# A rebuilt head for a fused attention and expert kernel: loads, first chunk, dummy matmuls and V copies

## The chip, the cores and the metric

The kernel runs on one core of a Trainium2 chip. The metric is the device time of one execution in microseconds (us). Names used below: TensorE (PE) multiplies matrices and writes PSUM, VectorE (DVE) and ScalarE (ACT) do elementwise work, GpSimd (POOL) does elementwise work in SBUF, and SyncE (SP) issues the DMAs.

## The reference

One sequence of S = 2048 tokens of width D = 448 passes a layernorm and a grouped attention (16 query heads of 28, one shared key and value head), and then a second layernorm and a block in which only the 8 tokens with the highest router score go through a gated feed-forward layer.

```python
q = (x @ wq).reshape(B, S, H, Dh).transpose(0, 2, 1, 3)      # x: layernormed, H = 16, Dh = 28
k = x @ wk                                                    # one key head for all 16
v = x @ wv
scores = jnp.einsum("bhqd,bkd->bhqk", q, k) * (Dh ** -0.5)
o = jnp.einsum("bhqk,bkd->bhqd", softmax(scores), v)
h = x0 + o.transpose(0, 2, 1, 3).reshape(B, S, H * Dh) @ wo   # x0: the input
...
r = xl @ w_r                                                  # xl = layernorm(h)
idx = jnp.argsort(-r)[:, :8]
y = (silu(x_sel @ w_gate) * (x_sel @ w_up)) @ w_down * sigmoid(r_sel)
out = h + xl + scatter_add(0, idx, y)
```

## The kernel before

The program is written as a graph of operations with reads, writes, an estimated duration and a priority. A planner (`_Graph.plan`) runs a list schedule over these estimates and so fixes, before anything runs, the order of the instructions on each engine. Each engine then works through its own list strictly in that order; semaphores hold an instruction until what it reads is there. A changed estimate, priority or dependency can therefore reorder all lists.

**Tiles.** x is 16 tiles of 128 tokens (`x_sb`), in four chunks of 512. For each chunk (`chunk(c)`, line 459) VectorE takes mean and variance of each tile (`bn_stats`, `bn_aggr`, lines 464 and 466), the reciprocal root is made (chunk 0: Ln and Exp on ScalarE, lines 471 and 473; others: a power on GpSimd, line 476), VectorE normalises four tiles (`xn`, line 479), TensorE transposes them in pairs (line 352), and the transposed chunk is copied from PSUM to `xnT` (lines 490, 493). Projections follow: K by `wk_rep` (the key weights four times side by side), copied into two versions `K[:, p]` (lines 501, 505), and V by `wv_pad`, copied into `Vs` in five scaled versions, one instruction each (line 516, with `vone` for a column of constants that sums the weights). Chunk 0 also projects Q of block 0 (`q_project`, line 450).

**Blocks.** A block b is 512 queries of 4 heads; there are 16. For each of the 16 key tiles j, a unit is two matmuls of Q and K into two PSUM banks, twice (p = 0, 1). In most tiles ScalarE takes the exponential of each unit (`act_unit`, line 753: `P`), in 57 of 256 tiles VectorE makes an approximation of it (`dve_unit` and `shift`, lines 766 and 772: `Y`). Matmuls with `Vs` add both into the block's accumulator. Block 0 has no VectorE tiles, blocks 4, 8 and 12 have three, the others four. ScalarE has two pairs of score banks to alternate on, and VectorE one, so a score matmul waits for the exponential two units earlier.

**Around the head.** SyncE issues, in this order: x tiles 0, 1 and 2, 3, then wk, wq, wv, x 4 to 15 in three loads, w_r, the three expert weights, and wo in four parts (which wait for each other). GpSimd fills `ident` (for the transposes), spreads wk, wq and wv into padded tiles (`wk_rep`, `wq_pad`, `wv_pad`, lines 391 to 402), and makes many constants. `last_w` (line 654) prepares products of wo and of the last x tiles with w_r, eight VectorE instructions of 448 columns, for the end of the kernel. At the end of a block VectorE copies the accumulator to `Ot` (line 551).

The same graph is also built a second time in an exact form that runs only when a flag asks for it.

Of the kernel before, what the change touches and what calls it, by code (L numbers as in the profile page):

```python
# [230 lines left out]
def _main(nc, G, sb, ps, psb, flag, scr, xs, A_x, A_wq, A_wk, A_wv, A_wo, B_w_r, B_w_gate, B_w_up, B_w_down, out,  # L231
# [13 lines left out]
    VC = (1.0, 1.6796875, 1.4140625, 1.1875, 1.0)  # L245
# [25 lines left out]
    vone = sb("vone", [128, NV, 4, 32], F32)  # L271
# [73 lines left out]
    def pk(b):  # L345
        return ("ps", b)
# [44 lines left out]
    G.op(PO, lambda e: e.memset(wk_rep[:, :, :], 0.0), 530, writes=["wk_rep"])  # L391
    for i in range(4):
        G.op(PO, lambda e, i=i: e.tensor_copy(wk_rep[0:CK, :, 32 * i:32 * i + DH], wk_sb[0:CK, :, :]), 300,
             reads=["wk_sb"], writes=["wk_rep"])
    G.op(PO, lambda e: e.memset(wq_pad[:, :, :, :], 0.0), 1800, writes=["wq_pad"])
    for ch in range(NCH):
        v = wq_pad[0:CK, ch, :, :].rearrange("p g (i c) -> p (g i) c", c=32)[:, :, 0:DH]
        G.op(PO, lambda e, ch=ch, v=v: e.tensor_copy(v, wq_sb[0:CK, ch, :].rearrange("p (h d) -> p h d", d=DH)), 590,
             reads=["wq_sb"], writes=["wq_pad"])
    G.op(PO, lambda e: e.memset(wv_pad[:, :, :], 0.0), 210, writes=["wv_pad"])  # L400
    G.op(PO, lambda e: e.tensor_copy(wv_pad[0:CK, :, 1:1 + DH], wv_sb[0:CK, :, :]), 280,
         reads=["wv_sb"], writes=["wv_pad"])
    G.op(PO, lambda e: e.memset(vone[:, :, :, :], 0.0), 500, writes=["vone"])
    for v in range(NV):
        G.op(PO, lambda e, v=v: e.memset(vone[:, v, :, 0:1], VC[v]), 100, writes=["vone"])  # L405
    G.prio = -1000
    G.op(PO, lambda e: e.memset(wo_pad[:, :, :], 0.0), 1600, writes=["wo_pad"])
# [35 lines left out]
    def head_bank(c):  # L443
        if c > 0:
            return MISC
# [584 lines left out]
```

## Time and profile before

| What | Value |
|---|---|
| Runs of the kernel | 444.52 us median of 3, from 441.43 to 445.93 |
| The profiled execution | 442.73 us |
| Its span (first to last instruction) | 441.3 us |
| TensorE busy | 357.1 us (81%) |
| VectorE busy | 366.5 us (83%) |
| ScalarE busy | 382.1 us (87%) |
| GpSimd busy | 46.8 us (11%) |
| DMA engines, mean busy share of the first three fortieths | 0.8, 0.9, 0.6 |

How to read the lines quoted below. In a timeline row stand start and length in us, engine, line of the kernel, operation, output and input, shapes and a count when like instructions are merged; in brackets the idle time of the engine just before and what ended it. In a group of the page the columns are count, then busy time and mean ns of one, then idle time before and its releasers. In a row of windows stand the stretch, its length, the busy time of each engine with the number of instructions, the granted TensorE clock (1.00 is full), the DMA share and GB/s. In a row of DMA issues stand the tile, the queue, the count, the size and the time from issue to landing. Releasers are inferred.

### The profile page before, as it was taken

To read this page: it belongs to the slowest core of one execution; us is meant where nothing else is said; L and a number is where in the kernel's file an instruction comes from. 1 tells how busy PE (TensorE), PEld (TensorE's weight loads), DVE (VectorE), ACT (ScalarE), POOL (GpSimd) and SP (SyncE) were. 2 spreads that over 40 slices of the span, in tenths; PEclk is the share of its full clock that TensorE was granted. 3 is DMA by queue.
4 is the path that set the end of the run, shared out by engine and by line. 5 is a ranking of instruction groups with operands and counts; after the bars stand their busy time and mean duration, and the time that the engine had idled before them with its cause. 6 is when DMAs were issued, how large, how long until landed. Compare 5 with 4: busy or idle time off the path is not lost.

```text
span 441.3 us, 7932 instructions
## 1 busy us (share of the span) xinstructions
PE 357.1 (81%) x3243; PEld 106.7 (24%) x3243; DVE 366.5 (83%) x792; ACT 382.1 (87%) x425; POOL 46.8 (11%) x76
## 2 busy tenths in 40 slices
PE   0888898888887988989887988888879879887754
PEld 0333212222222222222221222222222212221243
DVE  4999629989788899899986898999988899995371
ACT  1397689999998999999996999999989998996640
POOL 8210001010101101010102110101011010111000
PEclk9998769999999999999998999999999998998955
DMA  8960000000000030000000030000000200000010
GB/s 227 272 186 11 0 1 27 4 26 1 26 3 25 1 94 17 22 8 26 1 24 4 3 108 3 26 3 25 4 25 1 88 24 4 25 7 22 1 43 8
DMA packets 17350, 15.75 MB, mean 36 GB/s; under 512 B 5944, under 2 KB 14428, under 8 KB 17308
## 3 DMA queue, kind: packets, MB, share of 16 engines
q1 hardware_dynamic: 17212, 15.16, 11.8%
q8 instruction: 27, 0.44, 0.4%
q14 instruction: 15, 0.12, 0.1%
q0 software_dynamic: 96, 0.02, 0.0%
HBM read 11.70 MB, written 3.47 MB: 34 GB/s over the span
## 4 chain that ended last, share of the span: by engine, by line
DVE 31%; ACT 29%; PE 25%; DMA 9%; POOL 2%; issue 1%; SPq 1%; POOLq 0%; DVEq 0%
ACT P L753 29%; PE ps L349 25%; DVE Y L766 11%; DVE Y L772 8%; DMA Rb<-l_scr 5%; DVE Ot L551 2%; DMA xnT<-r 2%; POOL On L563 1%; DMA x_sb<-in_A_x_dram 1%; DMA l_scr<-Lc 1%; DVE xn L479 1%; DVE bn L464 1%; DVE K L505 1%; DVE xnT L493 1%; DVE Vs L516 1%
## 5 line engine op out<-in xcount | busy, mean ns | idle before, releaser
L753 ACT ACTIVATE P<-ps 128x1024 bf16<-128x1024 f32 x398 | 370.7, 1082 | 26.3 <-PE ps L349 25.0
L349 PE MATMUL ps<-Q,K 64*128 64x512 bf16 x1024 | 187.0, 394 | 44.0 <-ACT P L753 26.6
L766 DVE TENSOR_SCALAR Y<-ps 128x512 int16<-128x512 f32 x228 | 146.8, 680 | 24.9 <-PE ps L349 24.5
L772 DVE TENSOR_SCALAR Y<-Y 128x2048 int16<-128x2048 int16 x171 | 117.7, 724 | 1.5
L349 PEld LDWEIGHTS ps<-Q,K 64*128 64x128 bf16 x1024 | 44.6, 93 | 191.7 <-ACT P L753 141.4
L349 PE MATMUL ps<-P,Vs 128*32 128x512 bf16 x796 | 81.2, 399 | 0.3 <-ACT P L753 0.3
L349 PE MATMUL ps<-Y,Vs 128*32 128x512 bf16 x912 | 75.2, 387 | 0.5 <-DVE Y L772 0.3
L563 POOL TENSOR_TENSOR On<-Ot,Rb 128x512 bf16<-128x512 f32 x15 | 21.7, 1446 | 280.8 <-DMA Rb<-l_scr 280.8
L349 PEld LDWEIGHTS ps<-P,Vs 128*32 128x32 bf16 x796 | 20.6, 93 | 51.7 <-issue 50.4
L349 PEld LDWEIGHTS ps<-Y,Vs 128*32 128x32 bf16 x912 | 22.7, 96 | 22.8 <-issue 11.5
L349 PE MATMUL ps<-xnT,wq_pad 112*128 112x512 bf16 x64 | 21.8, 437 | 4.0 <-DVE Ot L551 3.5
L349 PE MATMUL ps<-wo_pad,On 128*128 128x448 bf16 (+1 forms) x64 | 18.0, 378 | 8.5 <-POOL On L563 7.7
L551 DVE COPY Ot<-ps 128x512 f32<-128x512 f32 x15 | 10.3, 688 | 8.0 <-PE ps L349 7.6
L456 DVE TENSOR_SCALAR Q<-ps,qone 128x512 bf16<-128x512 f32 x16 | 11.7, 730 | 5.9 <-PE ps L349 5.8
L352 PE MATMUL ps<-ident,xn 128*112 128x128 bf16 x64 | 6.3, 259 | 11.2 <-POOL vone L405 10.6
L464 DVE BATCH_NORM_STATS2 bn<-x_sb 128x6 f32<-128x448 bf16 x16 | 9.3, 602 | 4.4 <-DMA x_sb<-in_A_x_dram 4.4
L585 POOL TENSOR_TENSOR st<-st,nhalf 128x1 f32<-128x1 f32 x12 | 7.7, 641 | 48.1 <-DVE st L583 48.1
L579 DVE TENSOR_TENSOR hbuf<-ps,x_sb 128x448 f32<-128x448 f32 x12 | 7.4, 619 | 4.6 <-PE ps L349 4.5
L349 PEld LDWEIGHTS ps<-wo_pad,On 128*128 128x128 bf16 x64 | 4.7, 100 | 17.7 <-POOL On L563 8.8
L352 PEld LDWEIGHTS ps<-ident,xn 128*112 128x112 bf16 x64 | 5.2, 161 | 13.3 <-POOL vone L405 10.6
L598 DVE SCALAR_TENSOR_TENSOR junk<-hbuf,st,w_rb 128x448 bf16<-128x448 f32 x12 | 8.1, 677 | 0.0
L349 PEld LDWEIGHTS ps<-xnT,wq_pad 112*128 112x128 bf16 x64 | 4.4, 104 | 14.7 <-DVE Ot L551 7.0
(164 smaller groups left out, 158.8 us busy)
## 6 DMA issues: line engine op xcount, KB each, us to landing
Rb<-l_scr SPq DMA_DIRECT2D x15, 256.0 KB
wg_sb<-in_B_w_gate_dram SPq DMA_DIRECT2D x1, 1568.0 KB, 12.0
wu_sb<-in_B_w_up_dram SPq DMA_DIRECT2D x1, 1568.0 KB, 17.6
wd_sb<-in_B_w_down_dram SPq DMA_DIRECT2D x1, 1568.0 KB, 21.1
x_sb<-in_A_x_dram SPq DMA_DIRECT2D x3, 448.0 KB, 6.4
out_dram<-x_sb SPq DMA_DIRECT2D x3, 448.0 KB, 2.9
xn_scr<-xn SPq DMA_DIRECT2D x3, 448.0 KB, 3.9
x_sb<-in_A_x_dram SPq DMA_DIRECT2D x2, 224.0 KB, 2.9
```

Source lines behind the costliest of these rows:

```text
L349: return lambda e: e.matmul(o, lhsT=l, rhs=r, start=start, stop=stop)
L352: return lambda e: e.transpose(o, i, ident[0:p, 0:p])
L456: G.op(DV, lambda e: e.tensor_scalar(Q[:, b % 4, :], ps[:, bank, :], qone[:, 0:1], None, ALU.add), dvt(512), reads=[pk(bank), "qone"], wri ...
L464: G.op(DV, [lambda e, t=t: e.bn_stats(bn6[:, t, :], x_sb[:, t, 0:D])], dvt(D), reads=[("x", t)], writes=[("bn6", t)])
L551: G.op(DV, lambda e: e.tensor_copy(Ot[:, rb, :], ps[:, acc_bank(b), :]), dvt(512), reads=[pk(acc_bank(b))], writes=[("Ot", rb)], prio=u - 30)
L563: G.op(PO, lambda e: e.tensor_tensor(On[:, qb % 2, g, :], Ot[:, rb, :], Rb[:, rb, :], ALU.mult), 1270, reads=[("Ot", rb), ("Rb", rb)], wri ...
L579: G.op(DV, lambda e: e.tensor_tensor(hbuf[:, hr, :], ps[:, bank, 0:D], x_sb[:, t, 0:D], ALU.add), dvt(D), reads=[pk(bank), ("x", t)], writ ...
L585: G.op(PO, lambda e: e.tensor_tensor(st[:, t, 4:5], st[:, t, 7:8], nhalf[:, 0:1], ALU.pow), 570, reads=[("st7", t), "nhalf"], writes=[("st ...
L598: G.op(DV, lambda e: e.scalar_tensor_tensor(junk[:, :], hbuf[:, hr, :], st[:, t, 4:5], w_rb[:, :], ALU.mult, ALU.mult, accum_out=st[:, t, ...
L753: G.op(AC, lambda e: e.activation(P[:, sl, :, :], ps[:, b0:b0 + 2, :], ACT.Exp, bias=EBIAS, scale=OCT), 905, reads=[pk(b0), pk(b0 + 1)], w ...
L766: G.op(DV, lambda e, k=k: e.tensor_scalar(Y[:, n, 0, p + 2 * k, :].bitcast(I16), ps[:, 4 + k, :], 0.0, 32639.0 - 3 * STEP, ALU.max, ALU.mi ...
L772: G.op(DV, lambda e: e.tensor_scalar(Y[:, n, v, :, :].bitcast(I16), Y[:, n, 0, :, :].bitcast(I16), v * STEP, None, ALU.add), 610, reads=[( ...
```

## The change

The first stretch of the kernel is rewritten:

- **Loads.** x tiles 0 to 3 are four loads; then wk, wv and wq; x 4 to 15 wait until tile 3 has landed; wo (four parts, no longer one after the other), w_r and the expert weights wait until tile 15 has landed.
- **Weights.** `wk_rep` and `wv_pad` are cleared by VectorE and filled by ScalarE, in one instruction each; `wq_pad` is filled half by ScalarE and half by GpSimd.
- **Dummy matmuls.** 44 matmuls of `ident` by itself into bank 7, which nothing reads, are TensorE's first instructions.
- **Chunk 0** (`chunk0`) goes in halves of two tiles: Ln and Exp for each half on ScalarE, a transpose and a copy for each tile (half 0 on ScalarE, half 1 on VectorE), K and Q projections of 256 columns, the four K copies and the first Q copy on ScalarE.
- **Chunks 1 to 3.** One or two of four tiles are normalised on GpSimd (`nmean` serves it); chunk 1's root is made on ScalarE; PSUM banks 7, 4 and 5 take turns where bank 7 served alone.
- **V copies.** One instruction multiplies the projected values by the four constants `vcc`; the fifth copy, equal to the first, is gone; the column of constants is written once, on GpSimd.
- **Order.** Some priorities and estimates differ: Q of block 1 and the sum of w_r come later. The planner lays out all lists anew.

```diff
-    dma(x_sb[:, 0:2, 0:D], x_v[:, 0:2, :], [("x", t) for t in range(0, 2)], lat=2600.0)
-    dma(x_sb[:, 2:4, 0:D], x_v[:, 2:4, :], [("x", t) for t in range(2, 4)], lat=2600.0)
+    for t in range(4):
+        dma(x_sb[:, t, 0:D], x_v[:, t, :], [("x", t)], lat=2700.0 + 250 * t)
     dma(wk_sb[0:CK, :, :], A_wk.rearrange("(k p) n -> p k n", p=CK), ["wk_sb"], lat=4000.0)
-    dma(wq_sb[0:CK, :, :], A_wq.rearrange("(k p) n -> p k n", p=CK), ["wq_sb"], lat=6000.0)
-    dma(wv_sb[0:CK, :, :], A_wv.rearrange("(k p) n -> p k n", p=CK), ["wv_sb"], lat=6500.0)
+    dma(wv_sb[0:CK, :, :], A_wv.rearrange("(k p) n -> p k n", p=CK), ["wv_sb"], lat=4000.0)
+    dma(wq_sb[0:CK, :, :], A_wq.rearrange("(k p) n -> p k n", p=CK), ["wq_sb"], lat=5500.0)
     for i in range(4, NT, 4):
-        dma(x_sb[:, i:i + 4, 0:D], x_v[:, i:i + 4, :], [("x", t) for t in range(i, i + 4)], lat=6000.0)
+        dma(x_sb[:, i:i + 4, 0:D], x_v[:, i:i + 4, :], [("x", t) for t in range(i, i + 4)], lat=3500.0 + 400 * i,
+            reads=[("x", 3)])
...
-    G.op(PO, lambda e: e.memset(wk_rep[:, :, :], 0.0), 530, writes=["wk_rep"])
-    for i in range(4):
-        G.op(PO, lambda e, i=i: e.tensor_copy(wk_rep[0:CK, :, 32 * i:32 * i + DH], wk_sb[0:CK, :, :]), 300,
-             reads=["wk_sb"], writes=["wk_rep"])
+    G.op(DV, lambda e: e.memset(wk_rep[:, :, :], 0.0), 300, writes=["wk_rep"])
+    G.op(DV, lambda e: e.memset(wv_pad[:, :, :], 0.0), 100, writes=["wv_pad"])
+    G.op(AC, lambda e: e.activation(wk_rep[0:CK, :, :].rearrange("p k (i c) -> p k i c", c=32)[:, :, :, 0:DH],
+                                    wk_sb[0:CK, :, :].unsqueeze(2).broadcast_to([CK, NCH, 4, DH]), ACT.Identity),
+         500, reads=["wk_sb"], writes=["wk_rep"])
+    G.op(AC, lambda e: e.activation(wv_pad[0:CK, :, 1:1 + DH], wv_sb[0:CK, :, :], ACT.Identity), 200,
+         reads=["wv_sb"], writes=["wv_pad"])
     for ch in range(NCH):
...
+        if ch % 2:
+            G.op(AC, lambda e, v=v, w=w: e.activation(v, w, ACT.Identity), 480, reads=["wq_sb", "wq_pad"],
+                 writes=[("wq_pad", ch)])
+        else:
+            G.op(PO, lambda e, v=v, w=w: e.tensor_copy(v, w), 590, reads=["wq_sb", "wq_pad"],
+                 writes=[("wq_pad", ch)])
...
     for i in range(4):
-        dma(wo_pad[32 * i + 1:32 * i + 1 + DH, :, 0:D], wo_v[i], ["wo_pad"], lat=14000.0)
-    dma(w_rb[:, :], B_w_r.partition_broadcast(128), ["w_rb"], lat=14000.0)
+        dma(wo_pad[32 * i + 1:32 * i + 1 + DH, :, 0:D], wo_v[i], [("wo", i)], reads=[("x", NT - 1), "wo_pad"],
+            lat=6000.0)
+    dma(w_rb[:, :], B_w_r.partition_broadcast(128), ["w_rb"], reads=[("x", NT - 1)], lat=6000.0)
...
+    def v_project(c, bank):
+        pv = ps[:, bank, 0:128].rearrange("p (t c) -> p t c", c=32)
+        G.op(PE, [mm(pv[:, k, :], xnT[0:CK, c, ch, k * 128:(k + 1) * 128], wv_pad[0:CK, ch, :],
+                     ch == 0, ch == NCH - 1) for k in range(4) for ch in range(NCH)], 16 * 28,
+             reads=["wv_pad"] + xk(c), writes=[pk(bank)])
+        G.op(DV, lambda e: e.tensor_tensor(Vs[:, :, 4 * c:4 * c + 4, 1:32],
+                                           pv[:, :, 1:32].unsqueeze(1).broadcast_to([128, NV, 4, 31]),
+                                           vcc[:, :].unsqueeze(2).unsqueeze(3).broadcast_to([128, NV, 4, 31]),
+                                           ALU.mult), 620, reads=[pk(bank), "vcc"], writes=[("V", c)])
+
+    def chunk0():
+        G.prio = -500
+        for _ in range(44):
+            G.op(PE, mm(ps[:, 7, 0:128], ident[:, :], ident[:, :], True, True), 107, reads=["ident"], writes=[pk(7)],
+                 prio=-900)
+        for t in range(4):
...
+            if t % 2:
+                sl = slice(t - 1, t + 1)
+                G.op(AC, lambda e, sl=sl: e.activation(var[:, sl], mv[:, sl, 1], ACT.Ln, bias=EPS), 200,
+                     reads=[("mv", t - 1), ("mv", t)], writes=[("var", t // 2)])
+                G.op(AC, lambda e, sl=sl: e.activation(rstd[:, sl], var[:, sl], ACT.Exp, scale=-0.5), 200,
+                     reads=[("var", t // 2)], writes=[("rstd", -1 - t // 2)])
+        for h in range(2):
+            for t in (2 * h, 2 * h + 1):
...
+                if h == 0:
+                    G.op(AC, lambda e, src=src, dst=dst: e.activation(dst, src, ACT.Identity), 480,
+                         reads=[pk(t)], writes=[("xnT", 0, t)])
+                else:
+                    G.op(DV, lambda e, src=src, dst=dst: e.tensor_copy(dst, src), 340,
+                         reads=[pk(t)], writes=[("xnT", 0, t)])
+            c = slice(256 * h, 256 * h + 256)
+            x2 = [("xnT", 0, 2 * h), ("xnT", 0, 2 * h + 1)]
+            for kind in (("K", "Q") if h == 0 else ("Q", "K")):
+                bank = (4 if kind == "K" else 6) + h
+                G.op(PE, [mm(ps[:, bank, 0:256], wk_rep[0:CK, ch, :] if kind == "K" else wq_pad[0:CK, ch, 0, :],
+                             xnT[0:CK, 0, ch, c], ch == 0, ch == NCH - 1) for ch in range(NCH)], 4 * 115,
+                     reads=(["wk_rep"] if kind == "K" else wqk) + x2, writes=[pk(bank)])
...
+        v_project(0, 5)
+        G.prio = 9
+        q_project(1, MISC)
...
         for t in tl:
...
+            if t % 2 == 0 or t == 7:
+                G.op(DV, lambda e, t=t: e.tensor_scalar(xn[:, t, :], x_sb[:, t, 0:D], mv[:, t, 0:1], rstd[:, t:t + 1],
+                                                        ALU.subtract, ALU.mult), 310,
+                     reads=[("x", t), ("mv", t), ("rstd", c)], writes=[("xn", t)])
+            else:
+                G.op(PO, lambda e, t=t: e.tensor_scalar(xn[:, t, :], x_sb[:, t, 0:D], nmean[:, t:t + 1],
+                                                        rstd[:, t:t + 1], ALU.add, ALU.mult), 700,
+                     reads=[("x", t), ("nm", c), ("rstd", c)], writes=[("xn", t)])
...
-        for v in range(NV):
-            G.op(DV, lambda e, pv=pv, c=c, v=v: e.scalar_tensor_tensor(Vs[:, v, 4 * c:4 * c + 4, :], pv, VC[v],
-                                                                       vone[:, v, :, :], ALU.mult, ALU.add),
-                 dvt(128), reads=[pk(bank), "vone"], writes=[("V", c, v)])
```

More of the change, by code (lines that the diff above doesn't have):

```diff
@@ L400, in _main @@
[L400 to L403, printed above, removed]
+        w = wq_sb[0:CK, ch, :].rearrange("p (h d) -> p h d", d=DH)
+        if ch % 2:
[4 more added lines that the diff above has]
+                 writes=[("wq_pad", ch)])
@@ L404, in _main @@
+    wqk = [("wq_pad", ch) for ch in range(NCH)]
     for v in range(NV):
[L405 to L406 removed]
+        G.op(PO, lambda e, v=v: e.memset(vcc[:, v:v + 1], VC[v]), 100, writes=["vcc"])
+        G.op(PO, lambda e, v=v: e.memset(Vs[:, v, :, 0], VC[v]), 100, writes=["V1"])
+    G.prio = -300
     G.op(PO, lambda e: e.memset(wo_pad[:, :, :], 0.0), 1600, writes=["wo_pad"])
+    wok = [("wo", i) for i in range(4)]
@@ L615, in first_top @@
         first_row(bank)
-    old = [("xnT", 0), ("xnT", 1)]
+    old = xk(0) + xk(1)
     def first_row(bank):
@@ L675, in last_pre @@
             G.op(PE, fns[2 * p:2 * p + 2], 2 * 190,
-                 reads=[("On", 1, g) for g in range(3)] + ["wo_pad", "wo_hi", "wo_lo", "ident", ("x", t)],
+                 reads=[("On", 1, g) for g in range(3)] + ["wo_pad", "wo_hi", "wo_lo", "ident", ("x", t)] + wok,
                  writes=[pk(bank)])
```

161 lines of the change are left out of this document (86 added, 75 removed).

## The prediction

> **What bounds the kernel now.** I read the page first, for the engine that carries the span, then ScalarE's part of the timeline, then the timelines of VectorE and TensorE beside it, then windows with the granted clock.
>
> ```profile
> span 441.3 us, 7932 instructions
> ...
> L753 ACT ACTIVATE P<-ps 128x1024 bf16<-128x1024 f32 x398 | 370.7, 1082 | 26.3 <-PE ps L349 25.0
> ```
>
> ScalarE's 398 exponentials take 370.7 us, 0.931 us apart when nothing holds them (370.7 / 398; the 1082 ns of one overlap). So the span is the start of the first, plus 370.7, plus the gaps between them, plus what follows the last. The timeline of ScalarE gives start and gaps:
>
> ```profile
> 11.70 1.02 ACT L490 ACTIVATE xnT<-ps 112x1024 bf16<-112x1024 bf16 x1 [4.96 <-PE ps L352]
> 15.57 0.78 ACT L501 ACTIVATE K<-ps,kb,ksc 128x512 bf16<-128x512 f32 x1 [2.85 <-PE ps L349]
> 19.81 6.52 ACT L753 ACTIVATE P<-ps 128x1024 bf16<-128x1024 f32 x7 [3.46 <-PE ps L349]
> 26.61 2.16 ACT L753 ACTIVATE P<-ps 128x1024 bf16<-128x1024 f32 x2 [0.27 <-PE ps L349]
> 28.95 4.79 ACT L753 ACTIVATE P<-ps 128x1024 bf16<-128x1024 f32 x5 [0.17 <-PE ps L349]
> 33.99 1.94 ACT L753 ACTIVATE P<-ps 128x1024 bf16<-128x1024 f32 x2 [0.26 <-PE ps L349]
> 38.04 1.02 ACT L753 ACTIVATE P<-ps 128x1024 bf16<-128x1024 f32 x1 [2.11 <-PE ps L349]
> 39.26 2.97 ACT L753 ACTIVATE P<-ps 128x1024 bf16<-128x1024 f32 x3 [0.19 <-PE ps L349]
> 42.80 1.95 ACT L753 ACTIVATE P<-ps 128x1024 bf16<-128x1024 f32 x2 [0.57 <-PE ps L349]
> 45.28 1.94 ACT L753 ACTIVATE P<-ps 128x1024 bf16<-128x1024 f32 x2 [0.53 <-PE ps L349]
> 48.99 1.02 ACT L753 ACTIVATE P<-ps 128x1024 bf16<-128x1024 f32 x1 [1.77 <-PE ps L349]
> 50.21 1.94 ACT L753 ACTIVATE P<-ps 128x1024 bf16<-128x1024 f32 x2 [0.19 <-PE ps L349]
> 53.49 7.58 ACT L753 ACTIVATE P<-ps 128x1024 bf16<-128x1024 f32 x8 [1.34 <-PE ps L349]
> 61.88 2.11 ACT L753 ACTIVATE P<-ps 128x1024 bf16<-128x1024 f32 x2 [0.81 <-PE ps L349]
> 64.81 1.94 ACT L753 ACTIVATE P<-ps 128x1024 bf16<-128x1024 f32 x2 [0.82 <-PE ps L349]
> ...
> 406.52 6.88 ACT L753 ACTIVATE P<-ps 128x1024 bf16<-128x1024 f32 x7 [0.53 <-PE ps L349]
> ```
>
> The first exponential starts at 19.81. Block 0 has 32 of them (16 key tiles, two each, none on VectorE): 27 in the rows up to 50.21, and five of the eight at 53.49, so the 32nd is through at about 58.2. That is 38.4 us for 32 x 0.931 = 29.8 us of work: 8.6 us of gaps. They lie where a new chunk of keys is first needed (the 9th, 17th and 25th exponential: 27.5, 38.04, 48.99) and at 53.49. The last exponential ends at 413.4; the 27.9 us behind it is untouched by the change. VectorE, which makes the chunks, has no rest meanwhile:
>
> ```profile
> 20.18 1.30 DVE L479 TENSOR_SCALAR xn<-x_sb,mv,rstd 128x448 bf16<-128x448 bf16 x4
> 21.49 1.12 DVE L464 BATCH_NORM_STATS2 bn<-x_sb 128x6 f32<-128x448 bf16 x2
> 22.53 0.67 DVE L493 COPY xnT<-ps 112x1024 bf16<-112x1024 bf16 x1
> 26.39 1.49 DVE L505 TENSOR_SCALAR K<-ps,ksc,kb 128x512 bf16<-128x512 f32 x2
> 29.66 1.06 DVE L516 SCALAR_TENSOR_TENSOR Vs<-ps,vone 128x128 bf16<-128x128 f32 x5
> 59.51 0.69 DVE L551 COPY Ot<-ps 128x512 f32<-128x512 f32 x1 [5.82 <-PE ps L349]
> ```
>
> Its first idle time that matters is the 5.82 us before 59.51: until some 53 us VectorE sets the pace, ScalarE after that.
>
> **Term 1, the first exponential.** TensorE's projections of chunk 0 and the loads:
>
> ```profile
> 13.67 1.86 PE L349 MATMUL ps<-xnT,wk_rep 112*128 112x512 bf16 x4 [1.15 <-DVE mv L466]
> 21.43 0.65 PE L352 MATMUL ps<-ident,xn 128*112 128x128 bf16 x8
> 25.21 1.04 PE L349 MATMUL ps<-xnT,wk_rep 112*128 112x512 bf16 x4
> ...
> 0.72 0.95 SPq L363 DMA_DIRECT2D x_sb<-in_A_x_dram  x2
> 2.23 0.48 SPq L363 DMA_DIRECT2D wq_sb<-in_A_wq_dram  x1
> ...
> wq_sb<-in_A_wq_dram SPq DMA_DIRECT2D x1, 392.0 KB, 5.2
> ...
> wk_sb<-in_A_wk_dram SPq DMA_DIRECT2D x1, 24.5 KB, 4.1
> wv_sb<-in_A_wv_dram SPq DMA_DIRECT2D x1, 24.5 KB, 5.0
> ```
>
> SyncE spends 0.48 us on an issue. Four x loads end at 2.6, so wk is issued at 2.6, wv at 3.1, wq at 3.6; by the old times to landing they would be there at 6.7, 8.1 and 8.8. Nothing more lies ahead of them than before, when wq landed at 2.23 + 5.2 = 7.4, and x 4 to 15 now wait for tile 3; I take 6.3, 7.2 and 8.2. ScalarE's order is now: wk_rep, wv_pad, Ln and Exp of half 0, Ln of half 1, two wq_pad chunks, Exp of half 1, two xnT copies. A step that waits for a load holds all behind it. With 0.5 us for a copy of 448 to 512 elements (between half of the 1.02 and the 0.78 above) and 0.25 for a small one: wk_rep to 6.9, wv_pad 7.5, half 0's rstd 8.0, wq_pad 8.2 to 9.2, half 1's rstd 9.45, xnT 10.5. VectorE's xn and TensorE's transposes of half 0 fit in between.
>
> Then four half projections follow (K, Q, Q, K). A whole one took 1.86 us at 13.67 and 1.04 at 25.21; a half is 0.93 or 0.52. At the slow rate they end at 14.3; two K copies on ScalarE follow, and the first exponential is at 15.3. At the fast rate it is 13.65; with the late loads and the slow rate 16.1.
>
> Which rate holds? The page "TensorE: Matmul & The Clock Gate" of the Trainium skill (Part 1, and "Why this matters for your kernels") asks for about 4 us of matmuls to reach full rate, and says that an idle stretch of about 3 us loses it; by it the 44 dummies buy the 1.65 us if the rest between them and the projections stays short. The windows bear on this:
>
> ```profile
> 36.60:40.00 3.40, 1.98 (x28) 0.86 (x26) 3.40 (x7) 1.76 (x2) 0.00 (x0) 1.00 0.00 0
> 40.00:43.40 3.40, 3.27 (x20) 1.43 (x20) 3.40 (x11) 2.83 (x4) 0.00 (x0) 0.50 0.02 5
> ...
> 50.20:63.90 13.70, 12.51 (x57) 2.31 (x56) 2.58 (x7) 11.48 (x12) 0.00 (x0) 0.50 0.01 1
> ...
> 64.00:86.50 22.50, 19.54 (x180) 5.04 (x178) 21.21 (x49) 21.70 (x24) 1.70 (x1) 1.00 0.04 14
> ...
> 1.17 0.56 POOL L375 TENSOR_SCALAR ident<-idi 128x128 bf16<-128x128 int32 x1
> ```
>
> The numbers after the stretch and its length are PE, PEld, DVE, ACT, POOL, granted clock, DMA share and GB/s; the last row is of the timeline. After 3.4 us with TensorE busy 1.98, the granted clock is 0.50. The dummies run from 1.73 (when the last row's ident is done) for 44 x 0.08 to 0.12 us, that is till 5.3 to 7.0 (0.65 / 8; the slow end is half of a slow 256-column pass, 0.93 / 8). Till 10.55 only 16 transposes follow, 1.3 us of work in 3.5. I take the slow rate: **15.3, 4.5 us earlier**, with ends of 3.7 and 6.2. By the page's rule alone it would be 6.2.
>
> **Term 2, the gaps of block 0.** Chunk 1's Ln and Exp sit behind the 2nd and 3rd exponential on ScalarE (0.4 us on the path, new), so its rstd comes at 15.3 + 3 x 0.93 + 0.4 = 18.5. Then VectorE in the planner's new order: three xn (1.0; the fourth is on GpSimd), statistics (0.8), two xnT (1.2), Q of block 1 (0.7), small steps and one bn_stats (0.8), the V copy (0.65), bn_stats (0.6), first K copy (0.7): 25.0. With a score matmul and its semaphore the 9th exponential is at 25.7, against 27.5 before. ScalarE would have been ready at 15.3 + 8 x 0.931 + 0.4 = 23.15, so there is a gap of 2.5 there.
>
> Behind it VectorE has less to do per chunk: one V copy of 128x496 instead of five of 128x128. It is not in the trace; 0.65 is what a 512-column pass costs (1.49 / 2), less would be the five's 1.06 / 5, so it is 0.4 less than before, and at worst the same 1.06. One or two of four xn (0.33 each) go to GpSimd. What is decisive is the order: the new list has the Y steps of block 1 behind chunk 3, where the old had them between chunks (the row at 30.72 below is one). VectorE needs about 6 us from the first K copy of chunk 1 to that of chunk 2, some 31.7, including two of the wo-by-w_r products moved forward (row below); ScalarE needs chunk 2 at 25.7 + 7.4 = 33.1. Chunk 3 comes at 37.6 against 40.6. These two gaps (2.11 and 1.77) go.
>
> ```profile
> 30.72 1.27 DVE L766 TENSOR_SCALAR Y<-ps 128x512 int16<-128x512 f32 x2
> ...
> 67.53 0.62 DVE L656 SCALAR_TENSOR_TENSOR junk<-wo_pad,w_rb 128x448 bf16<-128x448 bf16 x1
> ...
> ...
> L563 POOL TENSOR_TENSOR On<-Ot,Rb 128x512 bf16<-128x512 f32 x15 | 21.7, 1446 | 280.8 <-DMA Rb<-l_scr 280.8
> ```
>
> New waits come instead. TensorE's list has four transposes in a row, two of them of tiles normalised on GpSimd (one tile between the 0.56 that 128 columns took for ident and the 1.45 of a two-input product of 512; if it goes by columns, 0.56 x 448 / 128 = 1.96; I take 0.9), and the scores of the next exponentials queue behind them: 0.4 us a chunk. Block 2's Q projection still blocks TensorE for 1.0 to 1.9, as at 53.49. The eight products of 0.62 now lie ahead of or among the first Y steps; from the first Y to the fifth unit VectorE needs 10.9 us (ten Y at 0.64, four shifts taken alike, a Q copy of 0.7, two products), beside 13 exponentials, 12.1 us. I put 2.0 for all this, between 0.5 and the 8.3 lost before from the 9th to the 32nd (58.2 - 27.5 - 24 x 0.931). So block 0 ends at 25.7 + 24 x 0.931 + 2.0 = 50.0: **8.2 us earlier** than 58.2, term 1 included.
>
> The four wo loads, w_r and the expert weights go behind x 15, about 12 us; the first user, the sum of w_r, is at some 31. SyncE is free again long before Ot of block 0. The POOL memsets that went (wk_rep, wv_pad, vone) hid under the loads.
>
> **Term 3, the rest.** The gaps of 0.81 and 0.82 at 61.88 and 64.81 belong to the stretch at clock 0.50; a full gain is 1.6, none is 0, I take 0.3. From block 2 on the new lists are nearly the old ones, so nothing else moves: 0, plus or minus 2.
>
> **Sum.** 8.2 + 0.3 = 8.5 us. The profiled execution took 442.73, so it would take 434.2. The median of the runs shown is 444.52, 1.8 above it (they reach from 441.43 to 445.93), so I predict **436.0**.
>
> **Rivals.** (a) The gain at the start is handed back at the chunks: the gaps after the 9th exponential stay at 8.3, and only 27.5 - 25.7 = 1.8 is left: 442.7. For it: VectorE was the pace until 53 us, and most of its work remains. Against: the Y steps leave its way. A late wq, with all of ScalarE's queue behind it, gives the same. 0.15.
> (b) The dummies hold the clock, or the loads are early: first exponential 13.65, all of chunk 1 1.6 earlier, only 0.5 of gaps later, and both gaps of term 3 gone: 8.2 + 1.6 + 1.5 + 1.6 = 12.9: 431.6. For it the page's rule above; against it the sparse 3.5 us. 0.18.
> (c) Slower: the clock of 0.50 falls into blocks 1 to 3. In the old kernel its 13.7 us fell at the end of block 0, where TensorE had 57 matmuls in it. A block at full clock has 19.5 us of TensorE in 22.5. A projection takes 1.86 / 1.04 = 1.79 times as long at half clock; midway between that and none, 1.4, makes 27.3, so each us at half clock loses 0.18. Beyond 48 us of it the gain is gone; 90 us would cost 16, net +7.5: 452.0. Against: from 63.9 on the clock was 1.00. 0.05.
>
> **Chances.** Forecast 0.62, (a) 0.15, (b) 0.18, (c) 0.05. About 1%, 4.4 us, is what can be told from no change. Faster: 0.60 of the forecast's and (b), 0.78. Within: (a) and the forecast's poor end, 0.17. Slower: 0.05. Range: 430.5 (all of (b) but its best) to 442.0 (into (a)).
>
> **What would show it.** First exponential near 15.3; chunk 0's half projections 0.93 or 0.52 long; the 9th exponential near 25.7 behind K; no gap of 2 us at the 17th and 25th; Ot of block 0 near 51; exponentials from 65 us on with gaps as before. Wrong, if ScalarE sits long on wq, if TensorE waits for xn of GpSimd, or if the clock is 0.50 beyond block 1.

## The result, and the profile after

The kernel after takes 429.53 us (median of 4, 426.39 to 435.08), the kernel before on the same chip 443.07 (median of 4, 441.43 to 445.93): 13.5 us less, 3.1%. The ratio, which leaves out executions that took over 1.5% more than the fastest of their kernel (here the one of 435.08), is 0.966, 95% interval 0.957 to 0.976. It is faster. The same kernel run again in another set (c_after below) gave 0.975 (0.968 to 0.981), so the size of the gain is known to about a per cent only. The profiled execution took 430.56 us against 442.73: 12.2 less.

The page of the kernel after, three lines (the first is the span, the second the packets of one instruction queue, the third the group of the exponentials; in the kernel before the group had 370.7 and 26.3):

```profile
span 428.6 us, 8035 instructions
...
q14 instruction: 14, 0.11, 0.1%
...
L823 ACT ACTIVATE P<-ps 128x1024 bf16<-128x1024 f32 x398 | 370.0, 1090 | 17.7 <-PE ps L350 16.4
```

The exponentials cost what they did; the idle time in front of them fell by 8.6 us. Where it went is seen in ScalarE's timeline of the kernel after:

```profile
7.71 1.04 ACT L405 ACTIVATE wq_pad<-wq_sb 112x448 bf16<-112x448 bf16 x2 [0.91 <-DMA wq_sb<-in_A_wq_dram]
...
14.07 1.02 ACT L525 ACTIVATE K<-ps,kb,ksc 128x256 bf16<-128x256 f32 x2 [1.17 <-PE ps L350]
14.99 1.94 ACT L823 ACTIVATE P<-ps 128x1024 bf16<-128x1024 f32 x2
...
20.48 2.87 ACT L823 ACTIVATE P<-ps 128x1024 bf16<-128x1024 f32 x3 [0.53 <-PE ps L350]
25.12 4.93 ACT L823 ACTIVATE P<-ps 128x1024 bf16<-128x1024 f32 x5 [1.76 <-PE ps L350]
30.38 5.72 ACT L823 ACTIVATE P<-ps 128x1024 bf16<-128x1024 f32 x6 [0.34 <-PE ps L350]
36.53 2.85 ACT L823 ACTIVATE P<-ps 128x1024 bf16<-128x1024 f32 x3 [0.43 <-PE ps L350]
39.73 21.19 ACT L823 ACTIVATE P<-ps 128x1024 bf16<-128x1024 f32 x23 [0.34 <-PE ps L350]
```

The row at 25.12 opens with the 9th exponential, the first that needs chunk 1. Behind it are three short gaps, before the 14th, the 20th and the 23rd, and then a long row without one (23 of it lie in this window); the 32nd, tenth of the last row, ends at 39.73 + 9 x 0.917 + 1.02 = 49.0. Set beside the kernel before:

| us | before | forecast | after | change |
|---|---|---|---|---|
| first exponential starts | 19.81 | 15.3 | 14.99 | -4.8 |
| 9th starts | 27.75 | 25.7 | 25.12 | -2.6 |
| 32nd ends (block 0) | 58.24 | 50.0 | 48.98 | -9.3 |
| 32nd to the end of the last | 355.2 | 354.9 | 353.8 | -1.4 |
| last to the end of GpSimd's last DMA instruction | 23.68 | the same | 23.67 | 0.0 |
| from there to the end of the span | 4.18 | the same | 2.18 | -2.0 |

The last column adds up to the 12.7 us by which the span is shorter (-9.3 - 1.4 - 2.0). The device time fell by 12.2 only: it is 1.4 us longer than the span before (442.73 against 441.3) and 2.0 longer after (430.56 against 428.6). It is so in every execution on record: 1.4 to 1.5 in all of the kernel before, 2.0 to 2.1 in all of the kernel after. So of the 2.0 us in the last row only some 1.5 reach the time.

The last row is the one that nothing in the forecast holds. These are the rows from which it is worked out, GpSimd's timeline of the kernel before and of the kernel after (start, length):

```profile
436.15 0.93 POOL L944 DMA_INDIRECT out_dram<-wq_sb,idxc  x1 [34.27 <-DVE wq_sb L943]
```
```profile
425.48 0.93 POOL L1014 DMA_INDIRECT out_dram<-wq_sb,idxc  x1 [34.12 <-DVE wq_sb L1013]
```

437.08 to 441.26 is 4.18; 426.41 to 428.59 is 2.18. No engine shows work in either stretch; the section on the last 2 us tells what lies there.

TensorE's timeline of the kernel after, the head:

```profile
1.79 4.28 PE L350 MATMUL ps<-ident 128*128 128x128 bf16 x44 [1.79 <-POOL ident L377]
7.19 0.74 PE L353 MATMUL ps<-ident,xn 128*112 128x128 bf16 x8 [1.12 <-DVE xn L493]
9.52 1.10 PE L353 MATMUL ps<-ident,xn 128*112 128x128 bf16 x8 [1.59 <-DVE xn L493]
10.41 1.06 PE L350 MATMUL ps<-xnT,wk_rep 112*128 112x256 bf16 x4
11.27 1.91 PE L350 MATMUL ps<-xnT,wq_pad 112*128 112x256 bf16 x8
12.97 1.06 PE L350 MATMUL ps<-xnT,wk_rep 112*128 112x256 bf16 x4
```

The dummies end at 6.07. The first transposes run at the full rate (0.74 for eight), the next, 1.6 us of rest later, do not (1.10), and all four half projections are slow: 0.96 to 1.06 for a half where a whole one took 1.86 or 1.04 before.

### The profile page after: what moved, and what is told of

The parts are those of the page before. It is cut to its first block, busy times and chain, and to the rows that moved or that the text cites. A ratio compares the mean times of both kernels' runs of the same rounds, so it can differ in the third digit from the quotient of the medians.

```text
span 428.6 us, 8035 instructions
## 1 busy us (share of the span) xinstructions
PE 354.1 (83%) x3295; PEld 111.2 (26%) x3295; DVE 364.6 (85%) x774; ACT 384.9 (90%) x438; POOL 45.5 (11%) x73
## 4 chain that ended last, share of the span: by engine, by line
DVE 34%; ACT 30%; PE 22%; DMA 10%; POOL 2%; issue 1%; SPq 1%; POOLq 0%; DVEq 0%; ACTq 0%
ACT P L823 29%; PE ps L350 22%; DVE Y L836 12%; DVE Y L842 9%; DMA Rb<-l_scr 5%; DMA xnT<-r 2%; DVE Ot L621 2%; POOL On L633 1%; DMA l_scr<-Lc 1%; DVE K L588 1%; DMA wq_sb<-in_A_wq_dram 1%; DVE Q L463 1%; DVE junk L668 1%; DVE xnT L581 1%; DMA Lc<-l_scr 1%
## 5 line engine op out<-in xcount | busy, mean ns | idle before, releaser
L350 PE MATMUL ps<-Q,K 64*128 64x512 bf16 x1024 | 184.9, 391 | 45.5 <-ACT P L823 30.0
L350 PE MATMUL ps<-P,Vs 128*32 128x512 bf16 x796 | 79.8, 393 | 0.0
L633 POOL TENSOR_TENSOR On<-Ot,Rb 128x512 bf16<-128x512 f32 x15 | 20.5, 1370 | 272.1 <-DMA Rb<-l_scr 272.1
L350 PEld LDWEIGHTS ps<-P,Vs 128*32 128x32 bf16 x796 | 20.6, 93 | 49.8 <-issue 49.6
L350 PE MATMUL ps<-xnT,wq_pad 112*128 112x512 bf16 (+1 forms) x68 | 20.2, 393 | 3.3 <-DVE Ot L621 3.3
L353 PE MATMUL ps<-ident,xn 128*112 128x128 bf16 x64 | 5.3, 236 | 3.0 <-DVE xn L493 2.7
L651 DVE BATCH_NORM_STATS2 bn<-hbuf 128x6 f32<-128x448 f32 x12 | 7.5, 624 | 0.1
L547 DVE BATCH_NORM_STATS2 bn<-x_sb 128x6 f32<-128x448 bf16 x12 | 6.9, 605 | 0.0
```

Of the source, the lines that this page charges most:

```text
L350: return lambda e: e.matmul(o, lhsT=l, rhs=r, start=start, stop=stop)
L547: G.op(DV, [lambda e, t=t: e.bn_stats(bn6[:, t, :], x_sb[:, t, 0:D])], 540, reads=[("x", t), ("mv", 4 * c - 1)], writes=[("bn6", t)])
L633: G.op(PO, lambda e: e.tensor_tensor(On[:, qb % 2, g, :], Ot[:, rb, :], Rb[:, rb, :], ALU.mult), 1270, reads=[("Ot", rb), ("Rb", rb)], wri ...
L651: G.op(DV, lambda e: e.bn_stats(bn6[:, t, :], hbuf[:, hr, :]), dvt(D), reads=[("h", hr)], writes=[("bn6", t)])
```

## The experiments

Three theories were to be told apart. **Order**: the gain in block 0 comes from where the planner puts the Y steps of block 1 on VectorE, behind chunk 3. **Less work**: it comes from VectorE's smaller share (V in one instruction, tiles on GpSimd). **Clock**: it comes from the dummies. Beside them stood the question of the last 2 us. None of the runs takes apart which piece of the new head brought the first exponential from 19.81 to 14.99. Eleven kernels ran; the times are in this table. "32nd" is the end of block 0's last exponential, "rest" from there to the end of the last, "at 0.50" the us at that granted clock within the rest, "end" the stretch behind GpSimd's last DMA instruction, all of the profiled execution. Medians are of 4 executions (6 in the last set, one for t_before92 and t_after36), ratios are to the kernel before on the same chip.

| kernel | first | 9th | 32nd | rest | at 0.50 | end | median (range) | ratio (95%) |
|---|---|---|---|---|---|---|---|---|
| before | 19.81 | 27.75 | 58.24 | 355.2 | 16.0 | 4.18 | 443.07 (441.43 to 445.93) | |
| after | 14.99 | 25.12 | 48.98 | 353.8 | 13.7 | 2.18 | 429.53 (426.39 to 435.08) | 0.966 (0.957 to 0.976) |
| a_no_dummy | 15.28 | 25.30 | 49.16 | 351.3 | 6.9 | 2.18 | 429.38 (428.25 to 432.03) | 0.973 (0.962 to 0.984) |
| a_one_bank | 12.89 | 26.66 | 53.45 | 354.0 | 16.3 | 2.28 | 435.03 (434.49 to 438.7) | 0.986 (0.974 to 0.998) |
| b_y_late | 18.86 | 27.49 | 52.32 | 355.9 | 17.0 | 4.29 | 436.70 (432.58 to 437.61) | 0.984 (0.973 to 0.996) |
| a_hole | 13.34 | 23.11 | 48.01 | 355.4 | 17.0 | 2.23 | 429.55 (428.43 to 431.27) | 0.970 (0.961 to 0.980) |
| a_v_split | 14.24 | 24.01 | 49.45 | 351.3 | 6.8 | 2.37 | 432.22 (428.75 to 434.44) | 0.983 (0.971 to 0.995) |
| a_dve_xn | 13.04 | 22.47 | 46.19 | 354.6 | 13.6 | 2.19 | 429.53 (428.63 to 431.89) | 0.977 (0.966 to 0.988) |
| a_pair_loads | 15.31 | 23.69 | 50.49 | 358.2 | 20.6 | 2.01 | 431.45 (428.87 to 436.15) | 0.978 (0.967 to 0.989) |
| t_before92 | 19.53 | 27.46 | 57.95 | 358.2 | 22.8 | 1.92 | 443.59 | |
| c_after | 15.12 | 25.15 | 49.00 | 351.7 | 10.2 | 1.88 | 430.58 (427.92 to 433.57) | 0.975 (0.968 to 0.981) |
| c_hole_xn | 13.21 | 22.43 | 46.15 | 354.4 | 13.6 | 2.00 | 427.81 (425.55 to 433.3) | 0.967 (0.959 to 0.974) |
| t_after36 | 15.23 | 25.51 | 49.37 | 353.3 | 10.2 | 4.31 | 432.29 | |

The median of before was 445.19 in the set of a_no_dummy, a_one_bank, b_y_late and a_hole, 442.96 in that of a_v_split, a_dve_xn, a_pair_loads and t_before92, and 443.94 in the last.

### Only the order: before, with the Y steps behind chunk 3

```diff
-        reads=[("Q", b % 4), ("K", j // 4, p)], ...
+        reads=[("Q", b % 4), ("K", j // 4, p), ("K", 3, 0)], ...
```

The edit is in `dve_unit` of the kernel before; nothing else differs.

> The kernel before with one dependency more: the score matmuls for VectorE's Y steps wait until chunk 3's keys are there, so the planner puts all Y steps behind chunk 3. Theory (order): the first exponential stays at 19.8, the gaps at the 17th and 25th exponential (2.11 and 1.77) go, the 32nd is through at 53 to 55 us instead of 58.2, and the total falls by 3 to 5 us, to 438 to 440. Rival (less work): VectorE has as much to do as before, and what leaves the chunks is missing when block 1 needs it; the total stays at 442 to 444 or rises.

ScalarE's timeline of b_y_late:

```profile
26.26 1.02 ACT L753 ACTIVATE P<-ps 128x1024 bf16<-128x1024 f32 x1 [0.30 <-PE ps L349]
27.49 9.30 ACT L753 ACTIVATE P<-ps 128x1024 bf16<-128x1024 f32 x9 [0.21 <-PE ps L349]
37.04 7.69 ACT L753 ACTIVATE P<-ps 128x1024 bf16<-128x1024 f32 x8 [0.25 <-PE ps L349]
```

The 17th exponential lies inside the row at 27.49, the 25th inside that at 37.04: the gaps of 2.11 and 1.77 are gone. One dependency brings block 0's end from 58.24 to 52.32. From the 9th exponential to there it takes 24.8 us, where the kernel before takes 30.5 and the kernel after 23.9: 5.7 of the 6.6 us that the whole change gains behind the 9th. The other 2.6 of the 9.3 are there at the 9th already.

The clock is a rival for a part of this. It was granted at 0.50 from 40.0 to 43.4 and from 50.2 to 63.9 in the kernel before, and at 1.00 throughout block 0 in b_y_late. The gaps of 2.11 and 1.77 lie outside those stretches, so they are not its doing; the one of 1.34 before the 28th (0.64 here) lies inside. Two things came out other than expected: the first exponential at 18.86 for 19.8 (a Q projection of the head took 1.25 where it took 1.87 in the kernel before), and the median, 8.5 us below the 445.19 of its set where 3 to 5 were expected. The spans of the two profiles differ by 5.2.

### The order taken back: after, with one bank

```diff
-        return (7, 4, 5)[hb[0] % 3]
+        return MISC
```

> The changed kernel with chunks 1 to 3 on PSUM bank 7 alone, as before the change; nothing else differs in the source, but the planner then puts VectorE's Y steps of block 1 between the chunks again. Theory (order): the first exponential stays at 15.0, the gaps at the 17th and 25th exponential come back, the 32nd is through at 53 to 55 us instead of 48.9, and the total is 433 to 436 us. Rival (less work): what closed the gaps is that VectorE has less to do for a chunk (one V copy, xn on GpSimd); then the 32nd is through near 50 and the total stays within 428 to 431.

With bank 7 alone for chunks 1 to 3 the planner lays out another order. VectorE's timeline of a_one_bank, rows of the K copies and Y steps:

```profile
23.67 0.67 DVE L836 TENSOR_SCALAR Y<-ps 128x512 int16<-128x512 f32 x1
24.35 0.66 DVE L836 TENSOR_SCALAR Y<-ps 128x512 int16<-128x512 f32 x1
25.14 1.53 DVE L588 TENSOR_SCALAR K<-ps,ksc,kb 128x512 bf16<-128x512 f32 x2
...
32.98 1.29 DVE L842 TENSOR_SCALAR Y<-Y 128x2048 int16<-128x2048 int16 x2
34.71 1.52 DVE L588 TENSOR_SCALAR K<-ps,ksc,kb 128x512 bf16<-128x512 f32 x2
```

Two Y steps stand ahead of the first K copy of chunk 1, more between the chunks. This execution had the earliest start of all (12.89) and block 0 still ended 4.4 us after that of the kernel after. The end of block 0 and the median lie where the order theory put them, but the way there was another. The gaps at the 17th and 25th, which were to come back, are 0.20 and 0.61. The loss is the 5.28 us ahead of the 9th, and there the Y steps did not hold the K copy up. It starts at 25.14, when TensorE's K projection of chunk 1 is through (23.22 + 1.89 = 25.11):

```profile
23.22 1.89 PE L350 MATMUL ps<-xnT,wk_rep 112*128 112x512 bf16 x4 [0.24 <-DVE xnT L581]
```

In the kernel after the same projection starts at 22.22 and takes 1.04. Two things differ here. The clock was granted at 0.50 from 18.42 to 32.07, where the kernel after had 1.00 from 15.5 on; and with one bank the second half of chunk 1's transposes came at 21.33, 2.7 us after the first, where the kernel after has them 0.6 apart. So this run does not part the order from the single bank and the clock. That order carries the larger part of the gain behind the 9th exponential rests on b_y_late alone.

### The dummies: left out, and filled up

The first kernel leaves out the 44 dummy matmuls (they compute nothing that is read). The second has 60 at the start and more between the steps:

```diff
+            for _ in range(24 if h == 0 else 4):
+                G.op(PE, mm(ps[:, 7, 0:128], ident[:, :], ident[:, :], True, True), 12,
+                     reads=["ident", ("xn", 2 * h + 1)], writes=[pk(7)])
             c = slice(256 * h, 256 * h + 256)
```

> The changed kernel without its 44 dummy matmuls. Theory (order): the first exponential was at 14.99 us although the granted clock was 0.50 during the projections, so the dummies buy nothing there: first exponential at 15.0 +-0.4, end of block 0's exponentials near 49, total 428 to 431 us, the same as the changed kernel. Rival (clock): the dummies shorten the first stretch where TensorE is slow, or decide when the clock comes back; without them the first exponential is at 16 or later and the total 2 us or more above 429.5.

> The changed kernel with 60 dummies instead of 44 at the start, 24 more between the transposes of the two halves of chunk 0 and 4 more between its projections, so that TensorE has hardly a rest from 1.8 us to the first scores. Theory (clock): the clock stays at 1.00 through the projections, the half projections of chunk 0 take 0.5 instead of 1.06 us each, the first exponential is at 13.4 to 14.2 instead of 14.99, the 9th 0.8 to 1.5 us earlier than 25.1, and the total 1 to 1.5 us lower. Rival: the clock falls all the same, or ScalarE's copies and not TensorE set the first exponential; it stays at 15.0 or later.

TensorE's timeline of a_no_dummy, and then of a_hole:

```profile
11.35 1.06 PE L350 MATMUL ps<-xnT,wk_rep 112*128 112x256 bf16 x4
12.20 1.69 PE L350 MATMUL ps<-xnT,wq_pad 112*128 112x256 bf16 x8
13.73 0.60 PE L350 MATMUL ps<-xnT,wk_rep 112*128 112x256 bf16 x4
```
```profile
7.92 1.50 PE L350 MATMUL ps<-ident 128*128 128x128 bf16 x24
9.69 0.73 PE L353 MATMUL ps<-ident,xn 128*112 128x128 bf16 x8 [0.26 <-DVE xn L493]
10.25 0.60 PE L350 MATMUL ps<-xnT,wk_rep 112*128 112x256 bf16 x4
10.69 0.60 PE L350 MATMUL ps<-xnT,wq_pad 112*128 112x256 bf16 x4
```

Without dummies the first exponential starts at 15.28 against 14.99, and the median is the same: the 44 as they stand buy nothing that the times show. Filled up, all projections run in 0.60, the first exponential is 1.65 earlier and the 9th 2.0, more than the 0.8 to 1.5 expected. At block 0's end 1.0 of that is left: behind the 9th the gaps add up to 2.3 where the kernel after has 1.1. The 1 to 1.5 us expected in the total are not seen in the median.

Whether the 44 alone hold the rate differs between the runs. The projections took 0.60 throughout in a_one_bank and a_dve_xn, and the first exponential came at 12.89 and 13.04; they were slow throughout in after, c_after and t_after36 (14.99 to 15.23), and in part in a_v_split and a_pair_loads.

### V in four instructions

```diff
-        G.op(DV, lambda e: e.tensor_tensor(Vs[:, :, 4 * c:4 * c + 4, 1:32], ...
+        for v in range(NV):
+            G.op(DV, lambda e, v=v: e.tensor_scalar(Vs[:, v, 4 * c:4 * c + 4, 1:32], pv[:, :, 1:32], VC[v], None,
```

> The V copy of each chunk as four copies of 128x4x31 again, the rest as in the kernel after. Order theory (the gain of the chunks comes from where the Y steps stand, and they stay behind chunk 3 here): four of about 0.21 us (1.06 / 5 in the kernel before) cost 0.85 instead of 0.68 a chunk, so the 9th exponential starts 0.2 to 0.5 us later than the 25.1 after, the 32nd ends at 49.0 to 50.0, and the median is 429 to 431. The rival, that VectorE's smaller work per chunk is what made the chunks early, wants 4 x 0.4 us or more: the 32nd at 51 or later, the median at 432 or above.

Block 0 ends at 49.45, inside the order theory's mark, but with an early start: the first exponential was at 14.24 and the 9th at 24.01, not later than 25.1. From the first exponential to the end of block 0 it takes 35.2 us instead of 34.0, so the one-step copy is worth about 1.2 us in block 0; with the start of the kernel after it would have ended at 50.2, between the two marks. The median of 432.22 lies above what the order theory gave, at the rival's value, but its four executions spread over 5.7 us, and the profiled one ended its span 1.8 us before that of the kernel after.

### All tiles normalised on VectorE

```diff
-            if t % 2 == 0 or t == 7:
+            if True:
```

> All 12 normalised tiles of chunks 1 to 3 made on VectorE instead of 7 there and 5 on GpSimd. VectorE gets 5 x 0.33 = 1.6 us more in block 0, and TensorE's transposes no longer wait for GpSimd (0.8 a tile). If the waits for GpSimd were a real cost (the 0.4 a chunk of the prediction), the 9th exponential stays at 25.1 or comes earlier and the gaps of 0.34 to 0.43 at the 17th and 25th go: the 32nd ends at 48.3 to 49. If they cost nothing, VectorE's extra work shows: the 32nd at 49.3 to 50.5. Either way the median is within 1.5 of 429.5.

GpSimd's timeline of the kernel after, what this edit takes away (the first row is of chunk 1, the second of chunk 2):

```profile
18.24 0.82 POOL L569 TENSOR_SCALAR xn<-x_sb,nmean,rstd 128x448 bf16<-128x448 bf16 x1 [7.74 <-ACT rstd L554]
...
23.39 1.41 POOL L569 TENSOR_SCALAR xn<-x_sb,nmean,rstd 128x448 bf16<-128x448 bf16 x2
```

This execution also started its exponentials 1.95 us early (all projections at 0.60, with the kernel after's own dummies). Its block 0 ended 2.8 earlier, ahead of both marks, so some 0.9 comes from the tiles. Most of that (0.7) lies ahead of the 9th exponential: the short gaps behind it did not go, they add up to 1.05 here and 1.11 in the kernel after. The next experiment removes the difference in the start.

### Both together, beside the kernel after once more

> The kernel after once more, so that it stands beside the other two of this set on the same chip. Median 428 to 431; in its profile the 32nd exponential ends at 48.0 to 49.2, the last at that plus 348 plus 0.45 us for every us at granted clock 0.50 in between (the line through the ten profiles so far), and the stretch behind GpSimd's last DMA instruction is 2.2. If that line is an accident of ten runs, the last exponential misses it by more than 1.5.

> The two edits that moved block 0's end earlier, together: dummies also between the transposes and the projections of chunk 0 (first exponential at 13.0 to 13.4 at the full clock) and all of chunks 1 to 3 normalised on VectorE (no wait for GpSimd). If the start and the waits for GpSimd add up, the 32nd exponential ends at 45.7 to 46.8, 2.2 to 3.3 before the kernel after, and the median is 426 to 428; if what is gained there is handed back later (by the clock or by VectorE's five more tiles), the median is the same as that of the kernel after within 1.

ScalarE's timeline of c_hole_xn, and TensorE's of c_after:

```profile
13.21 1.02 ACT L826 ACTIVATE P<-ps 128x1024 bf16<-128x1024 f32 x1
...
22.43 4.85 ACT L826 ACTIVATE P<-ps 128x1024 bf16<-128x1024 f32 x5 [1.55 <-PE ps L350]
27.61 8.45 ACT L826 ACTIVATE P<-ps 128x1024 bf16<-128x1024 f32 x9 [0.34 <-PE ps L350]
36.78 24.04 ACT L826 ACTIVATE P<-ps 128x1024 bf16<-128x1024 f32 x26 [0.71 <-PE ps L350]
```
```profile
7.42 1.10 PE L353 MATMUL ps<-ident,xn 128*112 128x128 bf16 x8 [0.75 <-DVE xn L493]
9.65 1.10 PE L353 MATMUL ps<-ident,xn 128*112 128x128 bf16 x8 [1.14 <-DVE xn L493]
10.55 1.06 PE L350 MATMUL ps<-xnT,wk_rep 112*128 112x256 bf16 x4
```

Block 0 ends at 46.15, 2.9 before c_after, and 1.9 before a_hole, whose start is the same within 0.13: the tiles on GpSimd, with the order that goes with them, cost 1.9 us in block 0 when the clock is open. The median is 2.8 us below that of c_after, on the same chip and in six executions each, but the intervals of the two ratios overlap: whether the total is better is not shown. The kernel after itself came out as expected (block 0's end at 49.00, 351.7 for a line that gave 348 + 0.45 x 10.2 = 352.6, and 1.88 at the end for 2.2).

### The loads in pairs

```diff
-    for t in range(4):
-        dma(x_sb[:, t, 0:D], x_v[:, t, :], [("x", t)], lat=2700.0 + 250 * t)
+    for t in (0, 2):
+        dma(x_sb[:, t:t + 2, 0:D], x_v[:, t:t + 2, :], [("x", t), ("x", t + 1)], lat=2700.0 + 250 * t)
...
-        dma(x_sb[:, i:i + 4, 0:D], ..., lat=3500.0 + 400 * i, reads=[("x", 3)])
+        dma(x_sb[:, i:i + 4, 0:D], ..., lat=3500.0 + 400 * i)
```

> x tiles 0 to 3 as two loads of two tiles, and the loads of x 4 to 15 no longer held until tile 3 has landed. SyncE issues the weights 0.96 us earlier (two issues of 0.48 fewer), but the larger x loads lie ahead of wq or beside it. The theory that wq's landing sets the start says: first exponential at 14.2 to 15.0 if wq lands earlier, 15.5 or later if x 4 to 15 take its bandwidth; and by the holes of the other runs (1.65 us at the start came to nothing in the total) the median stays at 428 to 431. The rival, that single tiles are what brought the start forward: first exponential at 16.5 or later, median 431 or more.

The first exponential started at 15.31, between the marks, and the median is 1.9 us above the kernel after's with overlapping ranges (the profiled execution, 436.15, was the longest of the four, so its 358.2 of rest is not typical). wq landed a little earlier (ScalarE begins `wq_pad` at 7.43 instead of 7.71), but VectorE's list has a statistics step of a later tile ahead of the first normalisation, and it waited for that load until 8.54. So the run says nothing on the size of the loads alone.

### The last 2 us

Two kernels run exactly what before and after run, and have more VectorE instructions in the exact form, which is jumped over:

```diff
+    for _ in range(92 if exact else 0):
+        G.op(DV, lambda e: e.memset(Lmn[:, :], 1.0), 90, writes=["Lmn"])
```

t_after36 has the same lines with 36 in the kernel after.

> The kernel before with 92 more instructions on VectorE in the second form of the program alone, which is jumped over; what runs is unchanged. VectorE's program grows from 2198 to 2290 instructions, 128 above the 2162 of the kernel after (128 of 64 bytes are the 8192 bytes of one instruction packet). If the 2 us at the very end come from where the last instructions lie in such a packet, the stretch from GpSimd's last DMA instruction to the end of the span falls from 4.2 to 2.2 us, and the span to about 439; if they come from something the program computes, it stays at 4.2.

> The kernel after with 36 more instructions on VectorE in the second, skipped form alone: 2162 + 36 = 2198 as in the kernel before. If the place of the last instructions sets the 2 us at the very end, the stretch behind GpSimd's last DMA instruction grows from 2.2 to 4.2 us; otherwise it stays at 2.2.

The page of t_before92, then of t_after36, with its span and the packets of the queue:

```profile
span 441.8 us, 7932 instructions
...
q14 instruction: 14, 0.11, 0.1%
```
```profile
span 430.7 us, 8035 instructions
...
q14 instruction: 15, 0.12, 0.1%
```

The kernel before has 15 packets there, the kernel after 14. With 92 more the end falls from 4.18 to 1.92 and a packet goes; with 36 more it grows from 2.18 to 4.31 and a packet comes. The count by itself proves little, as a_hole and a_v_split have 15 packets too, and ends of 2.23 and 2.37. The records of the last stretch say more. Behind the jump VectorE's list has two last steps, a drain and a semaphore step, which are not counted as work:

| kernel | drain starts, us behind GpSimd's last DMA instruction | semaphore step starts |
|---|---|---|
| before | 1.71 | 4.16 |
| b_y_late | 1.92 | 4.27 |
| t_after36 | 1.81 | 4.29 |
| after | 1.91 | 2.13 |
| t_before92 | 1.66 | 1.88 |

In the kernel before, a packet of 8192 bytes of that queue lies between the two, from 2.32 to 2.84; in the kernel after it comes at 2.66, behind both. In the kernel before the other four engines are through with their last steps 2.2 us ahead of VectorE. In t_after36 VectorE's last instruction ends at 430.67, those of the other four engines by 428.51. So the 2 us are one more fetch of VectorE's program behind the jump, between its last two steps; the computation has no part in it. (The span of t_before92 was not the expected 439, because its rest took 358.2.)

## Why the prediction fell short

The direction and the mechanism at the start and in block 0 were right; the gain was 12.7 us of the span where 8.5 was forecast, and the median of 429.53 fell 1.0 below the range. The 4.2 us between are 2.0 at the end, 1.1 in block 0 and 1.1 in the rest. Point by point:

**The step that failed** is in the first part: "the 27.9 us behind it is untouched by the change". It is 25.9 after. What the program computes there is untouched (23.68 against 23.67), but the 4.18 at its end were taken as part of that work, and half of them hung on where VectorE's last instructions lie. The change made VectorE's program 36 instructions shorter (the records hold 810 before and 792 after, 18 fewer, and the exact form is left with as many fewer), which moved the last ones to where they need one fetch less (92 more do the same). That is 2.0 of the 4.2 us of span that were missing, about 1.5 of them in the time. Without that fetch saved the median would have been about 431.0, inside the range.

**The step from the profile to the median** went wrong by more, and by chance. The forecast put the median 1.8 us above the profiled execution, as the three runs shown had it; after the change it was 1.0 below. That is 2.8 of the 6.5 us between 436.0 and 429.53. The profiled execution itself, 430.56 for the 434.2 forecast, is just inside the range, which begins at 430.5. So that the range was missed hangs as much on which executions fell into the median as on any term.

**Term 1** holds: 14.99 for 15.3. The slow rate was taken for the half projections, at 0.93; they took 0.96 to 1.06. wq was there at 7.7 for the 8.2 that was taken.

**Term 2** holds in its mechanism: the 9th exponential came at 25.12 for 25.7, and the gaps at the 17th and 25th went because of the order, which b_y_late shows; a_one_bank does not show it from the other side. One term was too large: "I put 2.0 for all this" came out at 1.5 in the prediction's own sum (49.0 - 25.12 - 24 x 0.931); the gaps that are seen make 1.1 (0.34 + 0.43 + 0.34). The term named the wait for GpSimd's tiles as the first part of it; those short gaps are as large without these tiles (1.05 in a_dve_xn). What the tiles cost in block 0, 0.9 us by a_dve_xn and 1.9 by c_hole_xn against a_hole, lies for 0.7 ahead of the 9th. The V copy took the 0.66 to 0.68 that was taken for it, though 1.49 / 2, from which it was said to come, is 0.75. The 9th before was at 27.75, not 27.5. Block 0's Ot came at 49.98 for 51.

**Term 3**, -0.3 plus or minus 2, measured -1.4. The rest of the program came out between 351.3 and 358.2 in the 13 profiles, and follows the us at granted clock 0.50 in it: a line of 348 plus 0.45 for each such us fits all within 1.4 (it was drawn through ten of them). By it the 2.3 us fewer give 1.0 of the 1.4. The kernel after run again had 351.7, so this part belongs to the execution more than to the change.

**Rivals.** (a) did not come: what is lost after the 9th is 1.5 by the same sum, not 8.3. (b) gave the better time (431.6 on the median) for the wrong reason: in the profile of the kernel after the dummies did not keep the rate, the first exponential was at 14.99 and not 13.65, and a_no_dummy loses nothing. That the rate can be held, and gives 13.3, a_hole shows. The windows of the kernel after:

```profile
5.30:8.70 3.40, 1.51 (x21) 1.17 (x19) 1.02 (x5) 2.26 (x8) 1.72 (x12) 1.00 1.02 312
8.80:12.20 3.40, 2.68 (x17) 2.18 (x18) 2.80 (x6) 1.70 (x5) 1.60 (x11) 0.50 0.63 198
```

After 3.4 us with TensorE busy 1.51 the clock is 0.50, as in the stretch that the prediction quotes; with the hole filled it stays at 1.00. The page "TensorE: Matmul & The Clock Gate" of the Trainium skill ("Why this matters for your kernels") asks for no idle gap of more than about 3 us if the rate is to be kept. In this trace that was not enough: the longest rest between the dummies and the projections was 1.59 us (the row of the second transposes), and the rate was lost, so here the measurement decides. (c) did not come: no stretch at 0.50 lies between 15.5 and 315.9. But its price of 0.18 for a us at half clock was too low, if the line above is a price.

## What to carry to other kernels

Where a list scheduler fixes the order, look first for work of the next stage that stands between the steps which the present stage waits for: one dependency that pushed it back gave 5.7 us, where the whole change gained 6.6 behind the 9th exponential. Warm-up matmuls are sure to help only if they reach to the work that is to be warm: of seven profiles with the 44, which end some 4 us ahead of the projections, two kept the rate throughout, and to leave them out cost nothing that the times show; 88 that filled the rests gave 1.65 us at the start. And a gain at the end of a span that no busy engine explains is best tried by moving the program without changing what runs.

## What the runs showed that was not expected

- Program length by itself moved the end of the span by 2.1 to 2.3 us, both ways (t_before92, t_after36). In the time it is less by about 0.5: between span and time lie 1.6 us in t_after36, 1.8 in t_before92, 1.4 to 1.5 in the kernel before and 2.0 to 2.1 in the kernel after.
- The granted clock of the profile does not tell the whole rate. In c_after it was 1.00 in every window from 1.8 to 15.7, and the half projections still took 1.06, where the same ones took 0.60 in a_dve_xn, whose list of TensorE begins with the same dummies. In the kernel before and in a_no_dummy it is 1.00 too while the first projections take 1.86 and 1.06: in these runs the column says nothing of the rate before its first change.
- The time behind block 0 goes with the us at clock 0.50 (0.45 for each, 13 profiles). That it is caused by them is not shown: in the kernel after ScalarE waited 2.60 and 0.41 us around the stretch at 0.50 from 315.9, and in c_after, without such a stretch there, 2.25 at the same place.
- 1.65 to 2.0 us at the start were not seen in the medians of a_hole and a_dve_xn (429.55 and 429.53, against 429.53 and 430.58 of the kernel after). Executions of one kernel differ by 3 to 10 us, so four of them cannot settle a gain of this size; whether it is handed back stays open.
